# Windowed attention and a SoLU feed-forward layer on one core: the feed-forward layer's middle tensor is transposed by DMA instead of by the tensor engine, its mean moves into the output weights, and the loads of q, k and v go ahead of the weights

## The chip, the cores and the metric

The kernel runs on one core of a Trainium2 chip. That core has five engines with queues of their own, which run in order and wait for each other by semaphores: TensorE (PE; its weight loads are listed apart as PEld), VectorE (DVE), ScalarE (ACT), GpSimd (POOL) and SyncE (SP), which here does nothing but issue DMAs. The metric is the device time of one execution in microseconds (us); lower is better.

## The reference

Attention over 4 batches x 8 heads, 768 positions, head dimension 64, in which a query sees the first 8 keys and the 96 keys up to its own; then a layer over the 3072 tokens, with d_model 512 and d_ff 1024:

```python
h = x @ w_in                               # x: attention output, 3072 x 512
e = np.exp(h - h_max)
sm = e / (np.sum(e, axis=-1, keepdims=True) + 1e-09)
solu = h * sm
mu = np.mean(solu, axis=-1, keepdims=True)
var = np.mean((solu - mu) ** 2, axis=-1, keepdims=True)
ln = (solu - mu) / np.sqrt(var + 1e-06) * g_ln
return (ln @ w_out).astype(np.float32)
```

## The kernel before

Everything is written as one Python program; a scheduler then puts the instructions of each engine into an order and inserts the semaphore waits. Tiles come from pools, and a tile's `bufs` says how many copies of it rotate; an instruction that writes a copy waits until the last reader of its old contents is done. Pools that are closed hand their memory to later pools, with the same kind of wait.

Three stages follow each other.

- **Weights** (lines 104 to 118). SP loads `w_in32` and `w_out32` (2 MB each, fp32) and the 1024 gains `g32`; DVE casts `w_in` to f16 and multiplies `w_out` by the gains in eight pieces (line 115). Both fp32 tiles are in the pool `wtmp`, which is closed before the attention's pools open.
- **Attention** (lines 122 to 298). Eight groups of four heads. Per group SP loads q, k and v (12 DMAs of 192 KB), ACT casts q and k (147, 149), PE transposes them into `pqQ` and `pqK` (157, 159), DVE copies these out (164, 165). `psg` (196, 201) are the scores against the global keys of four heads, `eg` their exponentials. Per head, `psb` (230) are the scores of the local band, `eb` their exponentials (ACT 238) times a mask (DVE 249), `psav` (263) the product with v, `rl` and `onrm` (279, 285) the division by the sum, `pxt` (291) a transpose, and `xT` (295) the copy into the transposed f16 input of the next stage. `psb` and `psg` share one PSUM buffer; `psav` and `pxt` share three.
- **Feed-forward** (lines 300 to 386). 24 tiles of 128 tokens. Per tile: `ph` = x @ w_in (8 matmuls, 313), `e` = exp (ACT 322) with its row sum `s0`, `solu` = e * (1024 / s0) * ph (DVE 328), its square sum (DVE 336), the subtraction of the mean (`smc`, DVE 342), eight PE transposes into `lT` (348), a copy out of PSUM (`lTs`, ACT 352), `po` = the product with the weights (8 matmuls, 355), and a copy of `po` into `ouall` (ACT 359). The normalisation is the same for a whole row, so it is put off: after the last tile the 24 columns of variances go through one square root and one reciprocal (361 to 378), and only then are the 24 tiles scaled (DVE 382) and stored by SP (386).

## Time before, and its profile

| | |
|---|---|
| runs | 334.45, 337.81 and 337.94 us, median 337.81 us |
| span of the profiled execution | 335.8 us |
| PE busy | 247.5 us, 74% of the span |
| DVE busy | 191.3 us, 57% |
| ACT busy | 144.8 us, 43% |
| POOL busy | 28.9 us, 9% |
| DMA | 29.65 MB, 88 GB/s over the span |

The span is the time from the first to the last instruction of one profiled execution; the timed median is 2.0 us longer than it. The stages are found in the trace by their first instructions: the first load of q at 18.94 us, the first `ph` matmul at 197.07 us, the first output store at 312.6 us.

### The profile page before, as it was taken

To read this page: it belongs to the slowest core of one execution; us is meant where nothing else is said; L and a number is where in the kernel's file an instruction comes from. 1 tells how busy PE (TensorE), PEld (TensorE's weight loads), DVE (VectorE), ACT (ScalarE), POOL (GpSimd) and SP (SyncE) were. 2 spreads that over 40 slices of the span, in tenths; PEclk is the share of its full clock that TensorE was granted. 3 is DMA by queue.
4 is the path that set the end of the run, shared out by engine and by line. 5 is a ranking of instruction groups with operands and counts; after the bars stand their busy time and mean duration, and the time that the engine had idled before them with its cause. 6 is when DMAs were issued, how large, how long until landed. Compare 5 with 4: busy or idle time off the path is not lost.

```text
span 335.8 us, 4686 instructions
## 1 busy us (share of the span) xinstructions
PE 247.5 (74%) x1760; PEld 140.0 (42%) x1760; DVE 191.3 (57%) x450; ACT 144.8 (43%) x179; POOL 28.9 (9%) x94
## 2 busy tenths in 40 slices
PE   0005797996969789798897887999889898895400
PEld 0002454664646466564664533444444444442100
DVE  1523364572756656364464528685965957865653
ACT  4012652536544363651634304655565656554100
POOL 7002101121101211110100000000000000000000
PEclk9999999999995755555555559999999999997755
DMA  7679966662777665368000000000000000000586
GB/s 273 227 143 217 196 125 126 127 127 47 142 143 141 142 126 107 60 133 164 2 0 0 2 0 0 2 0 2 2 0 2 0 0 2 0 0 1 197 302 250
DMA packets 81349, 29.65 MB, mean 88 GB/s; under 512 B 76720, under 2 KB 76720, under 8 KB 81328
## 3 DMA queue, kind: packets, MB, share of 16 engines
q1 hardware_dynamic: 81328, 29.37, 38.4%
q8 instruction: 13, 0.21, 0.3%
q14 instruction: 8, 0.07, 0.1%
HBM read 23.07 MB, written 6.29 MB: 87 GB/s over the span
## 4 chain that ended last, share of the span: by engine, by line
PE 49%; ACT 18%; DVE 16%; DMA 10%; issue 4%; SPq 2%; DVEq 0%; ACTq 0%
PE psb L230 13%; PE po L355 9%; PE psav L263 8%; ACT eb L238 7%; PE pxt L291 6%; DVE solu L328 6%; DMA out_dram<-osb 4%; DMA g<-in_moe_g_ln_dram 4%; ACT lTs L352 3%; PE pqK L159 3%; PE pqQ L157 3%; PE psg L196 3%; DVE sq L336 3%; ACT e L322 3%; PE ph L313 2%
## 5 line engine op out<-in xcount | busy, mean ns | idle before, releaser
L238 ACT ACTIVATE eb<-psb 128x1536 f16<-128x1536 f32 x32 | 46.4, 1451 | 52.0 <-PE psb L230 51.7
L230 PE MATMUL psb<-qTt,kTt 64*128 64x256 f16 x192 | 45.6, 395 | 18.9 <-ACT eb L238 15.0
L313 PE MATMUL ph<-w_in_sb,xT 128*128 128x512 f16 x192 | 49.9, 394 | 7.2 <-DVE solu L328 6.6
L355 PE MATMUL po<-gw_out_sb,lTs 128*128 128x512 f16 x192 | 48.4, 398 | 5.0 <-ACT lTs L352 3.8
L249 DVE TENSOR_TENSOR eb<-eb,bmask 128x1536 f16<-128x1536 f16 x32 | 30.5, 952 | 19.3 <-ACT eb L238 19.3
L230 PEld LDWEIGHTS <-kTt 64*128 64x128 f16 x192 | 22.0, 125 | 34.8 <-issue 26.5
L157 PE MATMUL pqQ<-ident,qq 128*128 128x128 f16 x96 | 14.9, 309 | 27.1 <-ACT qq L147 27.1
L355 PEld LDWEIGHTS <-lTs 128*128 128x128 f16 x192 | 17.9, 101 | 39.0 <-ACT lTs L352 20.1
L328 DVE SCALAR_TENSOR_TENSOR solu<-e,r,ph 128x1024 f16<-128x1024 f16 x24 | 30.7, 1280 | 2.7 <-DVE r L325 0.3
L322 ACT ACTIVATE e<-ph 128x1024 f16<-128x1024 f32 x24 | 24.6, 1027 | 15.7 <-PE ph L313 15.6
L359 ACT CAST ouall<-po 128x512 f16<-128x512 f32 x24 | 14.1, 586 | 36.7 <-PE po L355 36.7
L336 DVE CUSTOM_DVE_ANT_0 sq<-solu 128x1024 f16<-128x1024 f16 x24 | 29.2, 1216 | 0.0
L291 PE MATMUL pxt<-ident,onrm 128*64 128x128 f16 x192 | 26.1, 305 | 2.2 <-DVE onrm L285 2.1
L313 PEld LDWEIGHTS <-xT 128*128 128x128 f16 x192 | 18.4, 101 | 22.1 <-issue 5.5
L352 ACT COPY lTs<-lT 128x1024 f16<-128x1024 f16 x24 | 24.3, 1011 | 7.2 <-PE lT L348 7.2
L279 DVE RECIPROCAL rl<-psav 128x6 f32<-128x6 f32 x32 | 6.3, 196 | 33.5 <-PE psav L263 33.3
L263 PE MATMUL psav<-vo,eb 128*128 128x65 f16 x352 | 25.1, 243 | 0.0
L295 DVE COPY xT<-pxt 64x768 f16<-64x768 f16 x32 | 17.6, 549 | 12.7 <-PE pxt L291 12.6
L291 PEld LDWEIGHTS <-onrm 128*64 128x64 f16 x192 | 18.7, 159 | 14.2 <-DVE onrm L285 9.3
L263 PEld LDWEIGHTS <-eb 128*128 128x128 f16 x352 | 20.9, 130 | 7.8 <-issue 4.4
L147 ACT CAST qq<-qq 128x768 f16<-128x768 f32 x16 | 13.2, 824 | 22.7 <-DMA qq<-in_q_dram 22.7
L157 PEld LDWEIGHTS <-qq 128*128 128x128 f16 x96 | 9.4, 137 | 32.4 <-ACT qq L147 29.9
(63 smaller groups left out, 253.5 us busy)
## 6 DMA issues: line engine op xcount, KB each, us to landing
qq<-in_q_dram SPq DMA_DIRECT2D x32, 192.0 KB, 3.9
kk<-in_k_dram SPq DMA_DIRECT2D x32, 192.0 KB, 4.2
v<-in_v_dram SPq DMA_DIRECT2D x32, 192.0 KB, 3.8
out_dram<-osb SPq DMA_DIRECT2D x24, 256.0 KB, 2.0
w_in<-in_moe_w_in_dram SPq DMA_DIRECT2D x1, 2048.0 KB, 7.9
w_out<-in_moe_w_out_dram SPq DMA_DIRECT2D x1, 2048.0 KB, 13.9
g<-in_moe_g_ln_dram SPq DMA_DIRECT2D x1, 4.0 KB, 13.7
```

The source lines that it names most:

```text
L157: nc.tensor.transpose(out=pqQ[:, a, :], in_=qq16[:, a, :], identity=ident)
L230: nc.tensor.matmul(out=psb[:, cj, :], lhsT=kT[:, ts(cj, P)], rhs=qTp[:, ds(P * cj, NQB)], start=st, stop=not st,)
L238: nc.scalar.activation(out=eb.rearrange("p a f -> p (a f)"), in_=psb.rearrange("p a f -> p (a f)"), func=AF.Exp, scale=inv_sqrt_d,)
L249: nc.vector.tensor_tensor(out=eb.rearrange("p a f -> p (a f)"), in0=eb.rearrange("p a f -> p (a f)"), in1=bm_ap, op=ALU.mult,)
L263: nc.tensor.matmul(out=psav[:, rb, :], lhsT=lhs, rhs=rhs_ap, start=st, stop=last, tile_position=tp,)
L291: nc.tensor.transpose(out=pxt[0:D, rb, :], in_=onrm[:, rb, :], identity=ident,)
L313: nc.tensor.matmul(out=ph[:, ds(fh * 512, 512)], lhsT=xT[:, j, ts(tb, P)], rhs=w_in_sb[:, j, ds(fh * 512, 512)], start=(j == 0), stop=(j = ...
L322: nc.scalar.activation(out=e, in_=ph, func=AF.Exp, accum_out=s0)
L328: nc.vector.scalar_tensor_tensor(out=solu, in0=e, scalar=r, in1=ph, op0=ALU.mult, op1=ALU.mult, accum_out=s1,)
L336: nc.vector.tensor_tensor_reduce(out=sq, in0=solu, in1=solu, scale=1.0, scalar=0.0, op0=ALU.mult, op1=ALU.add, accum_out=s2all[:, tb : tb ...
L352: nc.scalar.copy(out=lTs, in_=lT)
L355: nc.tensor.matmul(out=po, lhsT=lTs[:, u, :], rhs=gw_out_sb[:, u, :], start=(u == 0), stop=(u == NFC - 1),)
```

## The change

- The loads of the first group's q, k and v come first on SP; the weights are loaded behind them, by a function that is called after that group's loads and transposes have been written down. `w_in` is now loaded by POOL's DMA queue, which casts to f16 on the way, so DVE's cast goes. `wtmp` is open beside the attention's pools.
- The mean is taken out of the weights instead of out of each token. After the gains are multiplied in (in fp32, in place), eight fp32 matmuls of `w_out32` with a matrix of 1/1024 (`meanw`) give every column's mean `pm`, and one DVE instruction over 128 x 4096 subtracts it and writes `gw_out_sb`. Each column of the weights then sums to zero over d_ff, so that a constant taken from a row of `solu` drops out of the product, and `smc` is not computed.
- Per tile, `u` = e * ph without the division; its square sum is taken by ACT (`sq`, line 353). `u` is transposed by one DMA issued by SP (`uT`, line 356): no transposes on PE, no copy `lTs` on ACT. The division by `s0` goes into the scale of the row.
- The tiles are taken in blocks of six (`GT`). After the sixth, four small DVE instructions and one POOL power (-0.5) give the six columns of scales `rs`. The second half of a tile (`ffn_out`: `po`, then ACT's scaled copy `osb`, then a store issued by ACT's DMA queue) runs six tiles behind the first.
- `ph` has three buffers instead of two, `uT` nine, `u`, `e`, `sq` and `osb` three each.

The diff, cut to its core (the removed lines stand in the functions above):

```diff
+    def load_weights():
+        w_out32 = wtmp.tile([P, NFC, D_MODEL], FP32, name="w_out32")
+        nc.sync.dma_start(out=w_out32, in_=moe_w_out.rearrange("(j p) c -> p j c", p=P))
+        g8 = wtmp.tile([NFC, P], FP32, name="g8")
+        nc.sync.dma_start(out=g8, in_=moe_g_ln.rearrange("(j p) -> j p", p=P))
+        nc.gpsimd.dma_start(out=w_in_sb, in_=moe_w_in.rearrange("(j p) f -> p j f", p=P))
...
+        nc.tensor.transpose(out=pg, in_=g8, identity=id8)
+        g32 = wtmp.tile([P, NFC], FP32, name="g32")
+        nc.vector.tensor_copy(g32, pg)
         for j in range(NFC):
             nc.vector.tensor_scalar_mul(
-                out=gw_out_sb[:, j, :], in0=w_out32[:, j, :],
+                out=w_out32[:, j, :], in0=w_out32[:, j, :],
                 scalar1=g32[:, j : j + 1],
             )
+        pm = apsum.tile([P, D_MODEL], FP32, name="pm", space=bass.MemoryType.PSUM,
+                        tag="out", bufs=3)
+        for j in range(NFC):
+            nc.tensor.matmul(out=pm, lhsT=meanw, rhs=w_out32[:, j, :],
+                             start=(j == 0), stop=(j == NFC - 1))
...
+        nc.vector.tensor_tensor(out=gw_out_sb, in0=w_out32, in1=pm_b,
+                                op=ALU.subtract)
...
+                if b == 0 and gi == 0:
+                    load_weights()
...
+        def ffn_in(tb, st):
+            i = tb % GT
+            ph = mpsum.tile([P, D_FF], FP32, name="ph", space=bass.MemoryType.PSUM,
+                            bufs=3)
...
+            nc.scalar.activation(out=e, in_=ph, func=AF.Exp,
+                                 accum_out=st[0][:, i : i + 1])
+            u = msb.tile([P, D_FF], FP16, name="u")
             nc.vector.scalar_tensor_tensor(
+                out=u, in0=e, scalar=1.0, in1=ph,
+                op0=ALU.mult, op1=ALU.mult, accum_out=st[1][:, i : i + 1],
             )
             sq = msb.tile([P, D_FF], FP16, name="sq")
+            nc.scalar.activation(out=sq, in_=u, func=AF.Square,
+                                 accum_out=st[2][:, i : i + 1])
+            uT = mut.tile([P, NFC, P], FP16, name="uT")
+            nc.sync.dma_start_transpose(out=uT, in_=u)
...
+            nc.gpsimd.tensor_tensor(out=rs, in0=t3, in1=nhalf, op=ALU.pow)
...
+        def ffn_out(tb):
+            uT = uTs.pop(tb)
+            po = mpsum.tile([P, D_MODEL], FP32, name="po", space=bass.MemoryType.PSUM)
+            for c in range(NFC):
+                nc.tensor.matmul(
+                    out=po, lhsT=uT[:, c, :], rhs=gw_out_sb[:, c, :],
+                    start=(c == 0), stop=(c == NFC - 1),
                 )
             osb = msb.tile([P, D_MODEL], FP32, name="osb")
+            nc.scalar.activation(out=osb, in_=po, func=AF.Copy,
+                                 scale=rss[tb // GT][:, tb % GT : tb % GT + 1])
+            nc.scalar.dma_start(out=out[ts(tb, P), :], in_=osb)
+
+        for n in range(NT + GT):
+            if n < NT:
+                if n % GT == 0:
+                    st = [stat.tile([P, GT], FP32, name=f"s{m}") for m in range(3)]
+                ffn_in(n, st)
+                if n % GT == GT - 1:
+                    rss[n // GT] = norm_scale(st)
+            if n >= GT:
+                ffn_out(n - GT)
```

Where the scheduler puts the moved instructions is not to be read from the diff. In the rows below, the names in brackets are what the instruction waits for: an engine, or one of the DMA lanes (DMAHW0 to 7) that the hardware queues' DMAs take in turn, so that every eighth DMA waits for the one eight before it.

On SP, at the start of the program, before:

```order
L108 DMA w_in_109<-in_moe_w_in_dram 128x4x1024
L111 DMA w_out_112<-in_moe_w_out_dram 128x8x512
L113 DMA g_114<-in_moe_g_ln_dram 128x8x1
L137 DMA qq_142<-in_q_dram 128x6x64 [waits DMAHW1_49,DMAHW2_49,DMAHW0_49,DVE_49]
L141 DMA kk_143<-in_k_dram 128x6x64
L137 DMA qq_142<-in_q_dram 128x6x64
```

and now, from the ninth DMA of that queue (the eight ahead of it are q, k and v, without a wait):

```order
L155 DMA qq_167<-in_q_dram 128x6x64 [waits DMAHW0_49]
L159 DMA kk_168<-in_k_dram 128x6x64 [waits DMAHW1_49]
L197 DMA v_196<-in_v_dram 128x6x64 [waits DMAHW2_49]
L197 DMA v_202<-in_v_dram 128x6x64 [waits DMAHW4_49,DMAHW3_49,Pool_49]
L109 DMA w_out_208<-in_moe_w_out_dram 128x8x512
L111 DMA g_210<-in_moe_g_ln_dram 8x128 [waits DMAHW5_49]
L155 DMA qq_412<-in_q_dram 128x6x64 [waits DMAHW6_49]
```

The first load of q waited for the whole weights stage, DVE's work included; now `w_out` is the thirteenth DMA and the gains the fourteenth.

On DVE, behind the first mask multiplication of head 0, before:

```order
L249 TENSOR_TENSOR eb<-eb,bmask 128x1536 [waits DVE_49,Activation_49]
L279 RECIPROCAL rl<-psav 128x6 [waits PE_49]
L285 TENSOR_TENSOR onrm<-psav,rl 128x384 [waits DVE_49]
L249 TENSOR_TENSOR eb<-eb,bmask 128x1536 [waits Activation_49]
L295 COPY xT<-pxt 64x768 [waits PE_49]
```

and now, in the same place, where the next row after the last is head 0's `rl`:

```order
L270 TENSOR_TENSOR eb<-eb,bmask 128x1536 [waits Activation_49] x2
L121 COPY g_219<-pg 128x8 [waits PE_49]
L123 TENSOR_SCALAR w_out_208<-w_out_208,g_219 128x512 [waits DMAHW4_49,DVE_49]
L123 TENSOR_SCALAR w_out_208<-w_out_208,g_219 128x512 x7
L270 TENSOR_TENSOR eb<-eb,bmask 128x1536 [waits Activation_49]
L205 COPY vg_411<-vo_443 8x65 [waits Pool_49]
L205 COPY vg_411<-vo_449 8x65 [waits Pool_49]
L134 TENSOR_TENSOR gw_out_sb<-w_out_208,pm 128x4096 [waits PE_49]
```

On PE, now, the end of head 2's `psb`, half of head 3's, and then head 0's `psav` (before, head 0's `psav` followed on head 1's `psb`, and no weights stood between):

```order
L251 MATMUL psb<-qTt,kTt 128x256 [waits Pool_49]
L119 MATMUL pg<-id_213,g_210 128x8 [waits DMAHW5_49]
L251 LDWEIGHTS kTt
L251 MATMUL psb<-qTt,kTt 128x256 [waits Activation_49]
L251 LDWEIGHTS kTt
L251 MATMUL psb<-qTt,kTt 128x256
L251 LDWEIGHTS kTt
L251 MATMUL psb<-qTt,kTt 128x256
L130 MATMUL pm<-w_out_208,meanw 128x512 [waits DMAHW4_49,DVE_49]
L130 MATMUL pm<-w_out_208,meanw 128x512 [waits DVE_49] x7
L284 LDWEIGHTS eb
L284 MATMUL psav<-vo_157,eb 128x65
```

The scores of the first four heads have moved ahead of the weights' arithmetic, and the rest of these heads behind it, on PE and on DVE.

On ACT, in the middle of the feed-forward stage, before:

```order
L322 ACTIVATE e,s_2872<-ph 128x1024
L359 CAST ouall<-po 128x512
L352 COPY lTs<-lT 128x1024
L359 CAST ouall<-po 128x512
L352 COPY lTs<-lT 128x1024
```

and now, one tile and the beginning of the next (the numbers of the tiles are n for `e` and `sq`, n - 6 for `osb` and the store):

```order
L345 ACTIVATE e,s_2516<-ph 128x1024 [waits PE_49]
L387 ACTIVATE osb<-po,rs 128x512 [waits DMAHW0_49,PE_49]
L389 DMA out_dram<-osb 128x512 [waits DMAHW6_49,Activation_49]
L353 ACTIVATE sq,s_2518<-u 128x1024 [waits DVE_49]
L345 ACTIVATE e,s_2516<-ph 128x1024 [waits PE_49]
```

ACT's order is now a fixed round of four steps in which `sq` of a tile stands between its `e` and the next tile's. PE alternates 8 `po` and 8 `ph` matmuls from tile 7 on.

## Rows read from the trace of the kernel before

**Rows 1.** The page's first line and its chain that ended last.

```profile
span 335.8 us, 4686 instructions
...
PE 49%; ACT 18%; DVE 16%; DMA 10%; issue 4%; SPq 2%; DVEq 0%; ACTq 0%
```

**Rows 2.** The chain in order of time: start us, us, what.

```profile
1.84 13.71 DMA g<-in_moe_g_ln_dram
15.65 3.27 DVE gw_out_sb L115 x8
...
56.23 1.45 PE psb L230 x6
...
197.07 3.61 PE ph L313 x8
200.83 1.12 ACT e L322 x2
...
208.18 1.73 PE po L355 x8
...
218.34 1.13 ACT e L322 x2
...
231.74 1.13 ACT e L322 x2
...
313.04 2.33 DMA out_dram<-osb
```

**Rows 3.** The timeline, start of attention: start us, us, instruction [idle before].

```profile
19.94 0.55 SPq L137 DMA_DIRECT2D qq<-in_q_dram  x1
...
28.37 0.84 SPq L137 DMA_DIRECT2D qq<-in_q_dram  x1
...
40.06 0.20 DVE L279 RECIPROCAL rl<-psav 128x6 f32<-128x6 f32 x1 [1.69 <-PE psav L263]
```

**Rows 4.** The page's DMA issues: KB each, median us from issue to landing.

```profile
qq<-in_q_dram SPq DMA_DIRECT2D x32, 192.0 KB, 3.9
...
w_in<-in_moe_w_in_dram SPq DMA_DIRECT2D x1, 2048.0 KB, 7.9
w_out<-in_moe_w_out_dram SPq DMA_DIRECT2D x1, 2048.0 KB, 13.9
```

**Rows 5.** Groups of instructions by form: busy us, mean ns of one | idle before.

```profile
L328 DVE SCALAR_TENSOR_TENSOR solu<-e,r,ph 128x1024 f16<-128x1024 f16 x24 | 30.7, 1280 | 2.7 <-DVE r L325 0.3
...
L322 ACT ACTIVATE e<-ph 128x1024 f16<-128x1024 f32 x24 | 24.6, 1027 | 15.7 <-PE ph L313 15.6
...
L285 DVE TENSOR_TENSOR onrm<-psav,rl 128x384 f16<-128x384 f32 x32 | 17.8, 555 | 0.8
...
L359 ACT CAST ouall<-po 128x512 f16<-128x512 f32 x24 | 14.1, 586 | 36.7 <-PE po L355 36.7
...
L322 ACT ACTIVATION_READ_ACCUMULATOR e<-ph 128x1 f32 x24 | 4.8, 200 | 0.0
L184 POOL MEMSET vo<- 128x6 f16 x32 | 3.7, 124 | 60.0 <-PE psav L263 60.0
...
L69 POOL TENSOR_SCALAR_AFFINE_SELECT bmask<-bmask 128x2048 f16<-128x2048 f16 x1 | 1.9, 1947 | 1.6 <-ACT bmask L66 1.6
```

**Rows 6.** The timeline at the second tile of the feed-forward stage.

```profile
203.16 1.02 ACT L322 ACTIVATE e<-ph 128x1024 f16<-128x1024 f32 x1 [1.22 <-PE ph L313]
```

**Rows 7.** The timeline's last arithmetic instruction.

```profile
332.19 0.49 DVE L382 TENSOR_SCALAR osb<-ouall,rstdall 128x512 f32<-128x512 f16 x1 [0.21 <-DMA out_dram<-osb]
```

**Rows 8.** The tile `osb`: what stores it, ns min/median/max of the issue.

```profile
L386 SPq DMA_DIRECT2D out_dram<-osb x24: 332/332/440, 312.6 to 332.7; - x24
```

**Rows 9.** Windows: stretch, length, busy us of PE, PEld, DVE, ACT, POOL; PEclk (1.00 is full); DMA.

```profile
118.00:197.00 79.00, 67.89 (x554) 44.05 (x553) 43.25 (x91) 33.20 (x31) 7.32 (x26) 0.50 0.33 63
197.00:202.00 5.00, 4.93 (x12) 1.79 (x13) 0.04 (x2) 1.11 (x2) 0.00 (x0) 0.50 0.00 0
202.00:302.00 100.00, 91.87 (x533) 42.64 (x531) 73.16 (x182) 57.13 (x89) 0.00 (x0) 1.00 0.00 1
```

More of the change, by code (lines that the diff above doesn't have):

```diff
@@ L298 @@
                     )
[L300 removed]
+    GT = 6
     with tc.tile_pool(name="mpsum", bufs=2, space=bass.MemoryType.PSUM) as mpsum, \
          tc.tile_pool(name="msb", bufs=3) as msb, \
[L303 to L310 removed]
+         tc.tile_pool(name="mut", bufs=GT + 3) as mut, \
+         tc.tile_pool(name="stat", bufs=3) as stat:
+        nhalf = stat.tile([P, GT], FP32, name="nhalf", bufs=1)
+        nc.gpsimd.memset(nhalf, -0.5)
+        uTs, rss = {}, {}
+        st = None
+        def ffn_in(tb, st):
+            i = tb % GT
+            ph = mpsum.tile([P, D_FF], FP32, name="ph", space=bass.MemoryType.PSUM,
+                            bufs=3)
             for j in range(NCC):
@@ L341 @@
-            smc = msb.tile([P, D_FF], FP16, name="smc")
-            nc.vector.tensor_scalar(
-                out=smc, in0=solu, scalar1=muall[:, tb : tb + 1], scalar2=LNSC,
-                op0=ALU.subtract, op1=ALU.mult,
-            )
-            lT = mpsum.tile([P, NFC, P], FP16, name="lT", space=bass.MemoryType.PSUM)
-            for u in range(NFC):
-                nc.tensor.transpose(
-                    out=lT[:, u, :], in_=smc[:, ts(u, P)], identity=ident
-                )
-            lTs = msb.tile([P, NFC, P], FP16, name="lTs")
@@ L352 @@
-            nc.scalar.copy(out=lTs, in_=lT)
-            po = mpsum.tile([P, D_MODEL], FP32, name="po", space=bass.MemoryType.PSUM)
-            for u in range(NFC):
-                nc.tensor.matmul(
-                    out=po, lhsT=lTs[:, u, :], rhs=gw_out_sb[:, u, :],
-                    start=(u == 0), stop=(u == NFC - 1),
-                )
-            nc.scalar.copy(out=ouall[:, tb, :], in_=po)
-        nc.vector.tensor_scalar_mul(out=s2all, in0=s2all, scalar1=1.0 / D_FF)
-        nc.vector.tensor_tensor(out=varall, in0=muall, in1=muall, op=ALU.mult)
```

83 lines of the change are left out of this document (28 added, 55 removed).

## The prediction

> **What bounds the kernel now.** I read the page's chain first, then the chain in order of time, which cuts the span of 335.8 us [rows 1] into four parts, and then asked in each part what ends last.
>
> Up to 18 us it is the weights. The gains, third DMA of SP, land at 15.55 us, DVE's eight scalings of `w_out` take 3.27 us more [rows 2], and only then does SP issue the first load of q; its third load goes out at 19.94 us [rows 3], where the third DMA of the queue went out at 1.84 us [rows 2]. PE does nothing until then. From there to 197.07 us is attention, a chain that alternates between PE, ACT and DVE (PE alone is 49% of the whole chain [rows 1]). From 197.07 us it is the feed-forward stage: `e` of every third tile starts 231.74 - 218.34 = 13.40 us after the last such one [rows 2], 4.47 us a tile, through ACT, DVE, PE and ACT again in turn. PE is busy for 91.9 of 100 us in it [rows 9]. From 313 us on it is the 24 stores, up to 335.8: the last scaling starts at 332.19 us [rows 7], and 3.1 us pass from its end to the span's. So feed-forward and stores together take 335.8 - 197.1 = 138.7 us, and that is where most of the change lies.
>
> **The start: 18 us earlier, most of it given back.** The loads go out 19.94 - 1.84 = 18.1 us earlier. The weights are now inside attention, on its path. I follow them.
>
> `w_out` takes the thirteenth place on SP, which was issued at 28.37 us [rows 3], so now at 10.3 us. Landing: 13.9 us, as it took beside `w_in` before [rows 4], so 24.2 us. It has `w_in` beside it again, from POOL's queue. Bounds: 7.9 us, what `w_in` took [rows 4], if it gets the larger share, so 18.2 us; and 13.9 + 3.9 us, if the loads ahead of it are still under way (a load of q takes 3.9 us [rows 4]), so 28.1 us. PE's `pg` waits for the gains behind it and DVE's copy of `pg` for PE, some 0.9 us, then come the scalings, the first of which lets `pm` start at 25.1 us.
>
> `pm` is eight fp32 matmuls of 512 columns, and the trace has none in fp32. In f16, eight of them take 1.73 us at the full clock and 3.61 us at the half [rows 2, 9]. Low end: nothing but the last one behind the last scaling, 28.6 us. High end: both operands are twice as wide, and if each has to be fed in halves, that makes four products, at half clock 14.4 us, so 39.5 us. I take 7 us, which is two products at the half clock or four at the full one: 32.1 us.
>
> Then the subtraction over 4096 columns with one operand in PSUM: 4 x 1.28 = 5.1 us by `solu` (1024 columns, also one operand in PSUM), or 4096/384 x 0.555 = 5.9 us by `onrm` [rows 5]. I take 5.1 us as the nearer in length. Head 0's `rl`, queued behind it on DVE, runs at 37.2 us, where it ran at 40.06 us [rows 3]: of 18.1 us, 2.9 are left. Bounds 33.7 - (24.2 - 18.2) = 27.7 us and 28.1 + 0.9 + 14.4 + 5.9 = 49.3 us.
>
> But some work has been done meanwhile. Before, 56.23 - 40.06 = 16.2 us passed from this `rl` to the first `psb` of group 1 [rows 2, 3]. Of that, two heads' `psb` (1.45 us each [rows 2]) are now done but for half of one, with their exponentials on ACT; on the other hand group 2's first q and k are now transposed in this stretch and not later. I take 14 us, so group 1's `psb` at 51.2 us, 5.0 earlier than before, plus some 1.6 us for the transposes that group 1 no longer has to do. The other seven groups hold the same instructions as before. The feed-forward stage then starts at 197.07 - 6.6 = **190.5 us**; with the bounds, 16 us earlier to 5 us later than before.
>
> **Feed-forward.** Gone for a tile: eight transposes on PE, `lTs` on ACT, `sq`, `smc` and three small instructions on DVE. Added: `sq` on ACT, a DMA transpose, ACT's issue of the store. What the units then need:
>
> PE: 16 matmuls, 2 x 1.73 = 3.46 us at the full clock [rows 2, 9].
>
> ACT: a round of `e`, `osb`, store, `sq`. `e` takes 1.03 us, and 0.2 us for its sum's read that overlaps by half: `solu`'s chain shows 1.12 us [rows 2, 5]. `u` (1.28 us, 0.09 for its sum, as `solu`) then runs on DVE, and `sq`, which I price as `e` since it has the same length and a sum too, waits for it. So a round is 1.12 + 0.05 + 1.37 + 0.05 + 1.12 = **3.7 us**, as long as `osb` and the store fit into the 1.4 us that ACT waits for `u`: `osb` as `ouall`, 0.59 us [rows 5], and the issue 0.33 us as on SP [rows 8] (or 0.84, as for a load among many [rows 3]), so 0.9 to 1.4 us; they fit. The round is above PE's 3.46, so this exchange between ACT and DVE becomes the bound, at 3.7 us instead of 4.47.
>
> The DMA transpose has no row. A tile of `u` is 256 KB; cut into the 256-byte rows of 128 x 128 blocks it is 1024 pieces. The nearest row is the load of q: 768 pieces of 256 bytes, of which SP issues one every 0.84 us [rows 3] and which lands after 3.9 us [rows 4]. So 1.1 us a tile in a stream, and some 5 us to landing. `uT` is wanted six tiles later, 22 us; `u` has three buffers, so the transpose also has to be done some 10 us after its issue. Both cover it: I cost it at nothing. Low end the same nothing; the high end is a rival below.
>
> The page "DMA: Bandwidth & Descriptors" of the Trainium skill (section "Latency and other measured facts") gives a measured 261 GB/s for a DMA transpose, by which I estimate 1.0 us a tile, and the sum would stay as it is; "Advanced Engine Details and Errata" of the Trainium skill (section "DGE: Hardware vs Software") speaks against the change, since it calls a transpose issued by a hardware queue, as here, the less efficient kind. No run here shows either yet.
>
> The sum from the stage's start: `e` of tile 0 at 3.8 us (200.83), of tile 1 at 6.1 us (203.16 [rows 6]; the matmuls are at the half clock there [rows 9]). Tiles 2 to 6 have no second half: ACT alternates `sq` and `e`, 2.24 us a tile, tile 6 at 17.3 us. The first block's scales come in here (`sq` of tile 5, two small DVE steps, POOL's power, `osb` of tile 0): tile 7 at 21.6 us. Then 16 rounds of 3.65 to 3.7, tile 23 at 80.5 us. Its `u` ends 2.5 us later, `sq` 1.2, two DVE steps 0.5, the power 0.6 (between 0.12 us for POOL's smallest instruction and 1.95 for a large one [rows 5]). Then six tiles are still to be scaled; two have their `po` ready, four follow at PE's 1.8 us, the last `osb` ends 8.2 us later. With the 3.1 us to the end, 80.5 + 4.8 + 8.2 + 3.1 = **96.6 us** against 138.7. Bounds: 94 us (shorter issue, no gap at the blocks) and 106 us (issue 0.84, the power 2 us at each block, `osb` at 0.7).
>
> **The sum.** 190.5 + 96.6 = 287.1 us of span; with the 2.0 us by which the median (337.8) is above the profiled span, **289 us**.
>
> **Rivals.**
>
> A. The forecast: 181 + 94 + 2 = 277 us to 202.5 + 106 + 2 = 310.5 us by the bounds, most likely 281 to 303: chance 0.72.
>
> B. The transposes flow slower than ACT's round. If the crossbar moves pieces smaller than 256 bytes at the load's 0.84 us / 768 = 1.1 ns a piece, pieces of 64 bytes make 4.5 us a tile: 24 x 4.5 + 6 before the first + 9 behind the last = 123 us, total 315 us. Chance 0.11.
>
> C. The same, further: pieces of 32 bytes make 9 us a tile, 24 x 9 + 15 = 231 us, total 424 us, slower than before. It decides from where 24 tiles, 15 us and 190.5 pass 335.8 us: 5.4 us a tile. For it speaks that nothing in the trace shows such a transfer, and that nothing of the store's large packets carries over; against it, that the queue holds one DMA per tile and that the pieces in `u` are contiguous. Chance 0.12.
>
> D. The clock. In attention's second half PE is busy for 67.9 of 79 us and has the half clock; at 202 us, after 4.93 busy us of 5, the clock rises [rows 9]. If it stayed at the half clock, a tile would take PE 2 x 3.61 = 7.2 us, 17 tiles 60 us more: 349 us. Against it: at that clock the feed-forward's PE has no gaps, and the one such stretch in the trace ended in the rise. Chance 0.03. That gaps lower PE's clock and steady work raises it is also what "TensorE: Matmul & The Clock Gate" of the Trainium skill says (section "HAM oscillation — how this bites in real kernels"); the trace agrees in the direction.
>
> E. The earlier loads gain nothing, since `pm` and the subtraction come later still: that is the far end of A's bounds and is counted there.
>
> **How the numbers follow.** The likeliest is A with 289 us. A's far ends and B hold the rest of the upper side: 278 to 320 us holds about 0.97 of A and more than half of B, 0.77 or so, and to reach further up would only buy the thin space before C. A measurement of this kernel tells about 1% from no change. Faster by over 1%, below 334.4 us: A and B, 0.83. Slower: C and D, 0.15. Between: 0.02.
>
> **What would show it.** First load at about 1 us; `w_out` landing near 24 us; a gap on PE between head 3's `psb` and head 0's `psav` in which only `pm` runs; `rl` of head 0 near 37 us; `ph` near 190 us; `e` every 3.7 us, with ACT waiting for DVE's `u` and not for PE or a DMA; DMA transposes landing some 5 us after issue; no stores after the end but the last six tiles'. It would be wrong if `po` waits for `uT` or `u` for a transpose (B, C), if ACT's issue of the stores holds up `sq`, if `pm` takes much more than 7 us, or if the granted clock in the second half is 0.50.

## The result, and the profile after

The changed kernel takes 286.14 us (median of 4 runs, 285.64 to 287.89) against 337.88 us (4 runs, 334.45 to 337.99): a ratio of 0.851 with a 95% interval of 0.845 to 0.857, or 51.7 us less. The forecast was 289 us with a range of 278 to 320. The profiled execution took 286.56 us, its span is 284.9 us. All readings below are from that one, and answer to the span of 335.8 us of before.

The page's first line, the shares of its chain, and three of its DMA issues (KB each, median us to landing; for the transpose, to landing only):

```profile
span 284.9 us, 4203 instructions
...
PE 62%; ACT 15%; issue 9%; DVE 7%; SPq 2%; DMA 2%; POOL 1%; POOLq 0%; ACTq 0%
...
out_dram<-osb ACTq DMA_DIRECT2D x24, 256.0 KB, 2.1
w_out<-in_moe_w_out_dram SPq DMA_DIRECT2D x1, 2048.0 KB, 14.5
...
uT<-u SPq DMA_TRANSPOSE x24, 3.1
```

PE now carries 62% of the chain, where it was 49% [rows 1], and the DMA transposes are in no step of it. The time went in three places. Each is the difference of two starts in the two traces:

| part | before | after | less |
|---|---|---|---|
| span's start to the first `e` (loads, attention) | 200.83 | 194.01 | 6.8 |
| first `e` to the 24th | 301.89 - 200.83 = 101.1 | 266.05 - 194.01 = 72.0 | 29.0 |
| 24th `e` to the span's end | 335.8 - 301.89 = 33.9 | 284.9 - 266.05 = 18.9 | 15.1 |

**The start.** The timeline of after, where [rows 2, 3] stood before (start us, us, engine, instruction, idle before it):

```profile
0.81 0.45 SPq L155 DMA_DIRECT2D qq<-in_q_dram  x1
...
10.15 4.45 SPq L109 DMA_DIRECT2D w_out<-in_moe_w_out_dram  x1
...
26.55 0.80 PE L251 MATMUL psb<-qTt,kTt 64*128 64x256 f16 x3 [1.25 <-ACT eb L259]
...
27.28 8.70 PE L130 MATMUL pm<-w_out,meanw 128*128 128x512 f32 x16
...
36.01 4.42 DVE L134 TENSOR_TENSOR gw_out_sb<-w_out,pm 128x4096 f16<-128x4096 f32 x1 [5.12 <-PE pm L130]
...
40.35 0.19 DVE L300 RECIPROCAL rl<-psav 128x6 f32<-128x6 f32 x1
...
52.64 1.44 PE L251 MATMUL psb<-qTt,kTt 64*128 64x256 f16 x6 [0.25 <-ACT eg L228]
```

The loads start 18 us earlier, but head 0's `rl` runs at 40.35 us, where it ran at 40.06 [rows 3]. The weights stand in between: `w_out` lands at 24.65 us, `pm` cannot start before 27.28, since half of head 3's `psb` is in front of it and waits for ACT; it takes 8.70 us, and DVE's subtraction 4.42 more. So at this point all of the 18 us is gone. Group 1's first `psb`, the last row, stood at 56.23 us [rows 2] and is 3.6 us earlier; by the start of the feed-forward stage 6.8 us are there again.

**The feed-forward stage.** A round is 3.445 us. The window from 220 to 260 us (length, busy us and instructions of PE, PEld, DVE, ACT, POOL, then PE's clock, DMA share, GB/s), and one round of ACT and DVE:

```profile
220.00:260.00 40.00, 40.00 (x187) 18.12 (x185) 14.60 (x30) 31.01 (x57) 2.65 (x2) 1.00 0.63 154
```

```profile
262.60 1.00 ACT L345 ACTIVATE e<-ph 128x1024 f16<-128x1024 f32 x1
...
263.60 0.68 ACT L387 ACTIVATE osb<-po,rs 128x512 f32<-128x512 f32 x1
263.73 1.22 DVE L348 SCALAR_TENSOR_TENSOR u<-e,ph 128x1024 f16<-128x1024 f16 x1 [2.21 <-ACT e L345]
264.30 0.34 ACTq L389 DMA_DIRECT2D out_dram<-osb  x1
...
264.99 1.06 ACT L353 ACTIVATE sq<-u 128x1024 f16<-128x1024 f16 x1 [0.72 <-DVE u L348]
...
266.05 1.00 ACT L345 ACTIVATE e<-ph 128x1024 f16<-128x1024 f32 x1
```

Two things have the same length. PE has no gap in 40 us, and its 16 matmuls of a tile take 2 x 1.73 = 3.46 us. ACT, in the order in which its instructions stand, starts `e`, then waits until DVE's `u` is there, then does `sq`: 1.13 to `u`'s start, 1.26 to `sq`, 1.06 to the next `e`, 3.45 us. In this trace the chain that ended last runs over PE's matmuls without a break from 190.26 to 226.94 us, and from the second block's scales on over ACT and DVE: at a block's border ACT waits for the power on POOL before `osb`, and there the round is 4.1 us.

```profile
228.77 0.69 ACT L387 ACTIVATE osb<-po,rs 128x512 f32<-128x512 f32 x1 [0.84 <-POOL rs L375]
```

The two are so nearly equal that the trace alone does not say which of them sets the round.

**The tail**, in the timeline:

```profile
270.15 1.32 POOL L375 TENSOR_TENSOR rs<-t,nhalf 128x6 f32<-128x6 f32 x1 [20.09 <-DVE t L373]
271.51 1.26 ACT L387 ACTIVATE osb<-po,rs 128x512 f32<-128x512 f32 x2 [1.92 <-POOL rs L375]
...
272.25 8.75 PE L382 MATMUL po<-gw_out_sb,uT 128*128 128x512 f16 x32 [2.59 <-ACT osb L387]
```

The last block's scales come at 271.5 us. Until then both buffers of `po` are full and PE waits 2.59 us; four tiles are still to be multiplied, and they take 8.75 us, 2.2 us a tile in place of 1.73. The granted clock is 0.50 from 272.8 to 276.2 us, behind PE's wait, and 1.00 after that; over the window from 260 us on it is 0.89.

### The profile page after: what moved, and what is told of

The parts are those of the page before. It is cut to its first block, busy times and chain, and to the rows that moved or that the text cites. A ratio compares the mean times of both kernels' runs of the same rounds, so it can differ in the third digit from the quotient of the medians.

```text
span 284.9 us, 4203 instructions
## 1 busy us (share of the span) xinstructions
PE 241.1 (85%) x1585; PEld 135.5 (48%) x1585; DVE 135.8 (48%) x291; ACT 146.7 (52%) x201; POOL 34.3 (12%) x100
## 3 DMA queue, kind: packets, MB, share of 16 engines
q1 hardware_dynamic: 101664, 27.28, 49.2%
## 4 chain that ended last, share of the span: by engine, by line
PE 62%; ACT 15%; issue 9%; DVE 7%; SPq 2%; DMA 2%; POOL 1%; POOLq 0%; ACTq 0%
PE psb L251 15%; PE psav L284 10%; PE ph L337 9%; PE pxt L312 8%; PE po L382 7%; ACT eb L259 7%; ACT e L345 4%; PE pqQ L175 3%; PE pm L130 3%; PE pqK L177 3%; PE psg L217 3%; ACT eg L228 2%; DMA qq<-in_q_dram 2%; DVE gw_out_sb L134 2%; DVE u L348 1%
## 5 line engine op out<-in xcount | busy, mean ns | idle before, releaser
L251 PE MATMUL psb<-qTt,kTt 64*128 64x256 f16 x192 | 47.3, 407 | 15.5 <-ACT eb L259 12.7
L348 DVE SCALAR_TENSOR_TENSOR u<-e,ph 128x1024 f16<-128x1024 f16 x24 | 29.3, 1222 | 45.0 <-ACT e L345 45.0
L382 PE MATMUL po<-gw_out_sb,uT 128*128 128x512 f16 x192 | 46.4, 390 | 3.7 <-ACT osb L387 3.7
L337 PE MATMUL ph<-w_in_sb,xT 128*128 128x512 f16 x192 | 46.4, 392 | 0.6 <-DVE xT L316 0.6
L382 PEld LDWEIGHTS <-uT 128*128 128x128 f16 x192 | 19.2, 100 | 28.0 <-issue 6.6
L353 ACT ACTIVATE sq<-u 128x1024 f16<-128x1024 f16 x24 | 25.4, 1058 | 10.7 <-DVE u L348 9.9
L312 PEld LDWEIGHTS <-onrm 128*64 128x64 f16 x192 | 19.4, 164 | 18.0 <-DVE onrm L306 12.1
L316 DVE COPY xT<-pxt 64x768 f16<-64x768 f16 x32 | 17.6, 549 | 17.4 <-PE pxt L312 17.2
L228 ACT ACTIVATE eg<-psg,gbias 128x768 f16<-128x768 f32 x8 | 7.2, 900 | 35.2 <-PE psg L222 35.2
L284 PEld LDWEIGHTS <-eb 128*128 128x128 f16 x352 | 20.6, 129 | 8.5 <-issue 4.8
L387 ACT ACTIVATE osb<-po,rs 128x512 f32<-128x512 f32 x24 | 16.2, 680 | 10.4 <-PE po L382 6.2
L203 POOL CAST vo<-v 128x384 f16<-128x384 f32 x32 | 17.3, 547 | 14.8 <-DMA v<-in_v_dram 14.7
L306 DVE TENSOR_TENSOR onrm<-psav,rl 128x384 f16<-128x384 f32 x32 | 17.8, 555 | 0.7
```

Source lines behind the costliest of these rows:

```text
L251: nc.tensor.matmul(out=psb[:, cj, :], lhsT=kT[:, ts(cj, P)], rhs=qTp[:, ds(P * cj, NQB)], start=st, stop=not st,)
L284: nc.tensor.matmul(out=psav[:, rb, :], lhsT=lhs, rhs=rhs_ap, start=st, stop=last, tile_position=tp,)
L306: nc.vector.tensor_tensor(out=onrm, in0=psav[:, :, 0:D], in1=rl_b, op=ALU.mult)
L312: nc.tensor.transpose(out=pxt[0:D, rb, :], in_=onrm[:, rb, :], identity=ident,)
L337: nc.tensor.matmul(out=ph[:, ds(fh * 512, 512)], lhsT=xT[:, j, ts(tb, P)], rhs=w_in_sb[:, j, ds(fh * 512, 512)], start=(j == 0), stop=(j = ...
L348: nc.vector.scalar_tensor_tensor(out=u, in0=e, scalar=1.0, in1=ph, op0=ALU.mult, op1=ALU.mult, accum_out=st[1][:, i : i + 1],)
```

## The experiments

Twelve kernels were run. All are edits of the changed kernel; e11 is e3b with one edit more, and e12 and e13 join edits of the others. The theory: (a) the round fell because PE lost its transposes and `po`, six tiles behind, waits for nothing; (b) the tail fell because the stores no longer stand in a row behind the last tile; (c) of the 18 us at the start most was lost to the fold of the mean. The rivals were that (b) brought nearly all, that the lag or the fold was worth nothing, or that ACT set the round.

| kernel | median us (range) | ratio to before, 95% interval |
|---|---|---|
| changed kernel | 286.14 (285.64 to 287.89) | 0.851 (0.845 to 0.857) |
| e1_pe_transpose | 295.36 (294.62 to 295.73) | 0.886 (0.880 to 0.893) |
| e2_no_fold | 281.68 (278.32 to 284.51) | 0.840 (0.828 to 0.853) |
| e3_stores_last | 285.63 (284.18 to 286.51) | 0.857 (0.850 to 0.864) |
| e4_weights_later | 285.30 (283.47 to 286.07) | 0.856 (0.849 to 0.863) |
| e3b_scale_at_end | 298.62 (297.81 to 299.60) | 0.891 (0.887 to 0.895) |
| e10_order_ahead | 279.84 (276.84 to 282.46) | 0.832 (0.825 to 0.839) |
| e5_sq_dve | 286.50 (284.76 to 287.20) | 0.854 (0.849 to 0.859) |
| e6_half_po | 271.33 (269.01 to 272.95) | 0.811 (0.805 to 0.817) |
| e7_gt3 | 282.16 (280.61 to 284.25) | 0.833 (0.827 to 0.838) |
| e11_lag_one | 309.63 (308.00 to 311.33) | 0.914 (0.908 to 0.919) |
| e12_no_fold_ahead_gt3 | 282.32 (280.80 to 283.28) | 0.832 (0.827 to 0.837) |
| e13_ahead_gt3 | 276.34 (275.96 to 277.00) | 0.815 (0.812 to 0.819) |

The kernel before scatters by 1 to 3% within a group of runs beside them (330.6 to 340.4 us over the three groups, with medians of 334.6, 335.1 and 338.6 us), the changed kernels by 0.4 to 2.2%, e2 the most; so differences among these are taken from their medians and from the traces, and one of 2 or 3 us between medians of different groups shows little by itself.

**e1: the transposes back on PE.**

```diff
+            lT = mpsum.tile([P, NFC, P], FP16, name="lT", space=bass.MemoryType.PSUM)
+            for c in range(NFC):
+                nc.tensor.transpose(out=lT[:, c, :], in_=u[:, ts(c, P)], identity=ident)
             uT = mut.tile([P, NFC, P], FP16, name="uT")
-            nc.sync.dma_start_transpose(out=uT, in_=u)
+            nc.vector.tensor_copy(out=uT, in_=lT)
```
(`ph` has two buffers instead of three, to make room in PSUM.)

> The changed kernel with the middle layer transposed on TensorE again (eight transposes of a tile into one PSUM tile, copied to SBUF by VectorE) in place of the DMA transpose; everything else, the folded mean and the store of each tile at once among it, stays. Theory: the feed-forward stage is set by TensorE at 3.455 us a tile (ph 1.73 + po 1.73), tied with the chain of e and u on ScalarE and VectorE at 3.445; eight transposes more, by the old kernel some 0.6 us a tile, come on top, so the round is 4.0 to 4.2 us and 24 tiles give 13 to 18 us: about 301 us (297 to 306). Rival, that the gain of the stage comes from the stores and the statistics and the transposes were covered all along: no more than 2 us, about 287.

It took 295.4 us, 9.2 more, just under the expected range. The window from 220 to 260 us, and three rows of one round:

```profile
220.00:260.00 40.00, 40.00 (x244) 19.50 (x242) 20.82 (x39) 29.48 (x53) 2.65 (x2) 1.00 0.18 68
```

```profile
228.20 1.02 ACT L345 ACTIVATE e<-ph 128x1024 f16<-128x1024 f32 x1
...
230.63 0.62 PE L357 MATMUL lT<-ident,u 128*128 128x128 f16 x8
...
232.16 1.02 ACT L345 ACTIVATE e<-ph 128x1024 f16<-128x1024 f32 x1
```

PE again has no gap, and the round is 3.96 us: 0.51 longer for eight transposes that take 0.62 us with the overlap at both ends. So the transposes were not covered, and the DMA transpose gives back what they cost PE. It is less than the 13 to 18 us expected: from first to last `e` 10.7 us were added, but the tail is 1.2 us shorter and the stage starts 1.1 us earlier. Of the 10.7, 4.2 fall on the first six steps from `e` to `e` (16.3 us for 12.1), where the third `ph` buffer is missing too; the two are not told apart there.

**e2: no fold.** `pm` and the subtraction go; DVE takes each tile's mean off `u` instead:

```diff
...
+            nc.vector.tensor_scalar(
+                out=uc, in0=u, scalar1=mu, scalar2=None, op0=ALU.subtract)
-            nc.sync.dma_start_transpose(out=uT, in_=u)
+            nc.sync.dma_start_transpose(out=uT, in_=uc)
```

> The changed kernel without the fold of the mean into the output weights: no fp32 matmuls pm and no subtraction at the start; VectorE takes each tile's mean and subtracts it before the DMA transpose. Theory: of the 18 us by which the loads come earlier, the fold's 8.7 us of fp32 matmuls and 4.4 us of subtraction give most back, since they stand ahead of heads 0 to 3's second half; without them the stage starts 8 to 12 us earlier, and the extra VectorE work (two passes of 128x1024 in f16, under 2 us a tile) stays below the round of 3.45: about 276 us (273 to 280). Rival, that the start is held by something else (the order of heads 0 to 3, the softmax's exponentials): within 3 us of the changed kernel, 283 to 289; second rival, that the mean's passes lengthen the round on VectorE: 290 or more with a round above 3.6 us.

281.7 us, between the theory's range and the first rival's; the round stayed at 3.445. The stage began 4.9 us earlier, not 8 to 12. Where the rest went is seen in the first `rl` of the first four head groups, of the changed kernel and of e2:

```profile
40.35 0.19 DVE L300 RECIPROCAL rl<-psav 128x6 f32<-128x6 f32 x1
...
58.25 0.20 DVE L300 RECIPROCAL rl<-psav 128x6 f32<-128x6 f32 x1 [1.69 <-PE psav L284]
...
77.03 0.20 DVE L300 RECIPROCAL rl<-psav 128x6 f32<-128x6 f32 x1 [0.64 <-PE psav L284]
...
95.36 0.20 DVE L300 RECIPROCAL rl<-psav 128x6 f32<-128x6 f32 x1 [0.80 <-PE psav L284]
```

```profile
29.22 0.19 DVE L289 RECIPROCAL rl<-psav 128x6 f32<-128x6 f32 x1
...
50.54 0.20 DVE L289 RECIPROCAL rl<-psav 128x6 f32<-128x6 f32 x1 [1.69 <-PE psav L273]
...
71.82 0.20 DVE L289 RECIPROCAL rl<-psav 128x6 f32<-128x6 f32 x1 [2.12 <-PE psav L273]
...
91.37 0.20 DVE L289 RECIPROCAL rl<-psav 128x6 f32<-128x6 f32 x1 [2.12 <-PE psav L273]
```

At the first `rl` e2 leads by 11.1 us, which is the price of the fold there; then by 7.7, 5.2 and 4.0, and by 2.7 at the fifth to the seventh group. It comes back to 4.9 only in the eighth: there PE's clock is 1.00 from 155.0 to 158.3 us in e2 and 0.50 in the changed kernel. Whether the edit or only this execution made it rise is not shown. Against the kernel before, e2's lead is 10.8 us at the first `rl` and between 9.6 and 11.7 at the seven others, so its groups take as long as before. It is the changed kernel's groups that are shorter, 17.9, 18.8 and 18.3 us against 21.3, 21.3 and 19.6. While PE waited for the weights and did `pm`, ACT and the loads got ahead, and PE then found its work ready, as far as the waits tell: in the changed kernel it waits for ACT's `eb` ahead of `psb` for 0.4 us between 58 and 95 us (the first row), and for 3.8 us between 114 and 155 (the second); e2 waits for 3.5 us between 51 and 91 (waits: us, times, longest).

```profile
PE psb L251 <- ACT eb L259: 0.4, 1, 0.4
...
PE psb L251 <- ACT eb L259: 3.8, 4, 1.5
```

```profile
PE psb L240 <- ACT eb L248: 3.5, 3, 1.5
```

**e4: the weights in the middle.** `load_weights` is called at `b == 2` in place of `b == 0`.

> The changed kernel with the loading, scaling and folding of the weights moved behind head group 2's start, in the middle of attention; the fold is kept. Theory: the 8.7 us of pm and the 4.4 us of subtraction leave the start, but TensorE has them at the half clock in attention (about 13.7 us); attention is held by the exponentials on ScalarE with TensorE partly idle there, so some of it is hidden: 276 to 286 us, 281 taken. Rival, that attention has TensorE as its bound: all 13.7 us come back and the time is 286 to 292 us.

285.3 us, within the changed kernel's scatter, and inside the theory's range only at its end. Its `rl` at the groups around the fold:

```profile
86.25 0.20 DVE L300 RECIPROCAL rl<-psav 128x6 f32<-128x6 f32 x1 [2.12 <-PE psav L284]
...
123.34 0.19 DVE L300 RECIPROCAL rl<-psav 128x6 f32<-128x6 f32 x1
...
141.24 0.20 DVE L300 RECIPROCAL rl<-psav 128x6 f32<-128x6 f32 x1 [1.69 <-PE psav L284]
...
160.03 0.20 DVE L300 RECIPROCAL rl<-psav 128x6 f32<-128x6 f32 x1 [0.64 <-PE psav L284]
...
176.11 0.20 DVE L300 RECIPROCAL rl<-psav 128x6 f32<-128x6 f32 x1 [0.93 <-PE psav L284]
```

The same pattern a second time, elsewhere. Up to 86 us e4 leads the kernel before by 15.3 to 17.7 us: nearly the whole of the earlier loads is kept as long as no weights are in the way. The group with the fold takes 37.1 us in place of 20.6, and the three after it 17.9, 18.8 and 16.1; the lead over before goes from 15.3 to -2.2 and back to 7.9 us. So it is the weights' scaling and fold, wherever they stand, that take the shift away, and the groups behind them return some of it.

**e3: the stores last.** `osb` is held and the 24 stores are written behind the loop.

> The changed kernel with every output tile held in SBUF and all 24 stores issued after the last tile. Theory: a store that follows its tile is free, and 24 stores in a row at the end cost what the kernel before showed from its last scaling to its end, 15 to 20 us less the 2 to 3 of the one store that ends the changed kernel: about 300 us (296 to 306). Rival, that the 16 DMA engines take the stores side by side, so only the issue counts (24 x 0.34 us on one queue): about 293 us or less.

285.6 us, and it says nothing on the theory: the scheduler put each store behind its `osb` again (at 220.16, 221.25 and 224.69 us, between ACT's steps of the running stage). It is a repeat of the changed kernel. The order of the source did not bind the scheduler here; a dependence of the data does. Hence the next one.

**e3b: scaling at the end, forced by the data.**

```diff
...
-            nc.scalar.activation(out=osb, in_=po, func=AF.Copy,
-                                 scale=rss[tb // GT][:, tb % GT : tb % GT + 1])
-            nc.scalar.dma_start(out=out[ts(tb, P), :], in_=osb)
+            raw = hold.tile([P, D_MODEL], FP32, name=f"raw{tb}")
+            nc.scalar.copy(out=raw, in_=po)
...
+        rs = norm_scale(st)
+        for tb in range(NT):
+            osb = msb.tile([P, D_MODEL], FP32, name="osb")
+            nc.vector.tensor_scalar_mul(out=osb, in0=raws[tb],
+                                        scalar1=rs[:, tb : tb + 1])
+            nc.sync.dma_start(out=out[ts(tb, P), :], in_=osb)
```

> e3_stores_last had its stores put back behind their tiles by the scheduler, so it tested nothing; here the data force them to the end. The unscaled output tiles are held in SBUF in f32, the row statistics are worked out once over all 24 tiles after the last one (as in the old kernel), and then VectorE scales and SyncE stores 24 tiles in a row. Theory: the old kernel took 22.8 us from its first scaling (313.04) to its end (335.8), against 3.9 us from the changed kernel's last scaling to its end, so about 19 us come back, less what ScalarE saves: about 304 us (299 to 309). Rival, that the old end was slow only because its VectorE scalings were and the stores run side by side: 292 us or less.

298.6 us, 12.5 more, just under the expected range. Its end in the timeline:

```profile
268.53 4.20 POOL L376 TENSOR_TENSOR rs<-t,nhalf 128x24 f32<-128x24 f32 x1 [108.60 <-DVE t L374]
272.77 1.28 DVE L399 TENSOR_SCALAR osb<-raw,rs 128x512 f32<-128x512 f32 x3 [4.32 <-POOL rs L376]
273.28 21.23 SPq L401 DMA_DIRECT2D out_dram<-osb  x24
...
293.67 0.49 DVE L399 TENSOR_SCALAR osb<-raw,rs 128x512 f32<-128x512 f32 x1 [0.22 <-DMA out_dram<-osb]
```

From the first scaling to the span's end (297.3) it is 24.5 us. In the kernel before it was 23.9: its first scaling runs at 311.95 us, and the 313.04 of the expectation is the first store on the chain [rows 2].

```profile
311.95 1.28 DVE L382 TENSOR_SCALAR osb<-ouall,rstdall 128x512 f32<-128x512 f16 x3
```

In both, DVE waits for stores to free its three buffers. So the row of stores costs what was thought, and (b) holds. But 12.5 and not 19 us come on top, because without the scales no `po` waits: the first scaling is there at 272.8 us, when the changed kernel still has four tiles to multiply.

**e11: `po` one tile behind.** e3b with `ffn_out(n - 1)` in place of `ffn_out(n - GT)`.

> e3b_scale_at_end with po written one tile behind ph in place of six; nothing else differs, since there no po waits for scales. Theory: the six tiles of lag are what keeps TensorE from waiting for a tile's own e, u and DMA transpose (2.3 us, then 1.3 of issue and 3.1 to landing, 6.7 us in all, against 1.7 us for one ph); with one tile of lag the scheduler can put at most the third ph buffer in between, so a round grows from 3.45 to 4 to 5 us: 310 us or more (308 to 330), where e3b took 298.6. Rival, that the lag is worth nothing and the gain of the round comes from the transposes alone: 297 to 301.

309.6 us, 11.0 more than e3b. From first to last `e` it takes 82.8 us, e3b 71.4. The waits of PE and of its weight loads from 215 to 265 us (us, times, longest):

```profile
PE po L383 <- DMA uT<-u: 1.6, 6, 0.4
```

```profile
PEld L383 <- DMA uT<-u: 7.4, 11, 0.9
```

e3b has no wait of either kind there. The transpose lands 3.1 us after its issue here, 3.0 in e3b. So it is free only because several tiles lie between `u` and `po` (six here; e7 below tries three); the change's order of the work is about as much of the gain as the transposes that left PE. Neither e1 nor e11, with 82.8 us each from first to last `e`, comes back to the 101.1 of the kernel before; what the work that left DVE and ACT (`smc`, `lTs`, the small steps) gave was not run by itself.

**e5 and e6: ACT or PE?** e5 gives `sq` back to DVE; e6 lets `po` take four of eight matmuls (half of the sum over the middle layer is left out of its output).

```diff
-            for c in range(NFC):
+            for c in range(NFC // 2):
...
```

> The changed kernel with the square sums taken on VectorE again, as in the old kernel; ScalarE then has 1.06 us a tile less in the feed-forward stage. Theory: TensorE (3.455 us a tile) sets that round by itself, so only the first seven tiles, where ScalarE alternates e and sq at 2.04 us a tile, can gain: 283 to 287 us. Rival, that the chain over ScalarE and VectorE (3.445) is what holds TensorE: round down to some 2.6 us and 268 us or less.

> The changed kernel with four of the eight po matmuls of each tile left out (half of the sum over the middle layer is missing from the output), so TensorE has 2.6 us a tile in place of 3.455. Theory: ScalarE's and VectorE's round of 3.445 is tied with TensorE's and holds alone as well: the stage stays within 2 us, and only the six po at the end shorten, by 6 x 0.9 us: 279 to 284 us. Rival, that TensorE alone set the round: down to what the e and sq need on ScalarE, 2.0 to 2.7 us a tile plus the stores, 268 us or less.

e5 took 286.5 us with a round of 3.45 in its steady part: relief for ACT alone buys nothing. PE has no gap there from 220 to 260 us, and now `e` does wait for PE, 31.7 us in all, where it was 9.5 in the changed kernel:

```profile
L345 ACT ACTIVATE e<-ph 128x1024 f16<-128x1024 f32 x24 | 24.6, 1024 | 32.3 <-PE ph L337 31.7
```

e6 took 271.3 us, at 2.8 us a tile: under the theory's 279 to 284 and over the rival's 268. The theory fell, but the trace shows that more than PE's work changed:

```profile
228.22 1.01 ACT L345 ACTIVATE e<-ph 128x1024 f16<-128x1024 f32 x1
...
229.78 1.03 ACT L345 ACTIVATE e<-ph 128x1024 f16<-128x1024 f32 x1
...
230.78 1.07 ACT L353 ACTIVATE sq<-u 128x1024 f16<-128x1024 f16 x1
...
232.20 1.06 ACT L353 ACTIVATE sq<-u 128x1024 f16<-128x1024 f16 x1 [0.26 <-DVE u L348]
...
233.82 1.01 ACT L345 ACTIVATE e<-ph 128x1024 f16<-128x1024 f32 x1
```

With a shorter PE the scheduler ordered ACT anew: two `e`, then two `sq`, so that DVE's `u` runs beside the second `e`, and two tiles take 5.6 us, with ACT busy for 37.7 of the 40 us from 210 to 250. ACT's chain is 3.45 us only in the order that the changed kernel has; in another order it needs 2.8. The bound that no order removes is therefore PE's 3.46, by e5, e6 and e1 together; e6 alone does not show what the old order of ACT would have done with less on PE.

**e7: blocks of three.** `GT = 3` in place of 6.

> The changed kernel with blocks of three tiles for the statistics in place of six, so that po runs three tiles behind ph. Theory: the tail of the changed kernel (18.85 us from the last e to the end) holds a wait of TensorE for the last block's scales: with two po buffers it stands still 2.59 us before 272.25, and six tiles are left to scale when the scales come at 271.5; with three tiles left the tail loses 3 to 5 us, and four more of POOL's powers (1.32 us) run beside other work: about 282 us (280 to 284). Rival, that three tiles of lag no longer hide the DMA transpose (1.3 us of issue, 3.1 to 5.6 to landing, behind 2.3 of e and u) or that the block borders hold up ScalarE: 287 us or more.

282.2 us, 4.0 less, as expected; but the trace gives the edit a smaller part. The power takes 0.85 us on three columns instead of 1.32 on six, fewer tiles are left behind it, and from the 24th `e` to the end it is 278.9 - 267.37 = 11.5 us in place of 18.9. Of these 7.3 us, first to last `e` takes back 4.9 (76.9 us for 72.0), since `ph` runs only three tiles ahead and there are twice as many block borders. So stage and tail are 2.4 us shorter. The other 3.6 us of this execution lie ahead of the stage, which starts at 190.43 us (first `e`), where the order of PE is unchanged: PE's clock was 1.00 there from 50 to 56 us and 0.84 from 105 to 110, where the changed kernel's trace shows 0.50. Three tiles of lag still hide the transpose but for 3.0 us of waiting weight loads.

**e10, e12, e13: the order in attention.** From e2 came the idea that the order of PE's instructions makes the groups between 40 and 95 us short. e10 writes the next group's loads, casts and transposes ahead of the present group's heads, and its global block ahead of the last head:

```diff
...
+            for op, i in [('p', 0), ('h', 0), ('p', 1), ('h', 1), ('h', 2), ('g', 0), ('h', 3)]:
+                if op == "h":
+                    head(state, eg, i)
+                elif nxt and op == "p":
+                    prep(nxt, i)
+                elif nxt:
+                    eg2 = glob(nxt)
...
```

> The changed kernel with the same work, written in another order: each head group's loads, casts and transposes ahead of the heads of the group before, and its global block (psg, eg) ahead of the last head of the group before. The fold stays at the start. Reason: the lead of e2_no_fold over the changed kernel shrank from 11.1 us at the first rl to 2.7 at the fifth group, because the changed kernel's groups between 40 and 114 us took 18.3 to 18.8 us and those of e2_no_fold 19.6 to 21.3; on TensorE the two have the same instructions in another order (two scores in a row, psb twice, in the slow groups). Theory: the order is the cause, and with the interleaved order in all groups the last four, now 20.9 to 21.3, take 18.5, so about 10 us less: 276 us (272 to 281). Rival, that the period is set by the work or by the loads: 284 to 288.

279.8 us, 6.3 less, and the stage starts 5.8 us earlier; but the reason given is not borne out. From `rl` to `rl`, its groups in the middle take 18.4, 20.1, 19.9, 20.1 and 19.9 us, no 18.5. Short are the first such step (16.2 us), for which the preparation had been done while the weights were under way, and the last (15.7), in which no next group is to be prepared. In the last one the clock rises too, behind a stretch in which PE has no gap (windows as above):

```profile
155.00:160.00 5.00, 5.00 (x45) 3.34 (x44) 3.26 (x8) 2.17 (x2) 0.00 (x0) 0.51 0.01 3
160.00:165.00 5.00, 3.33 (x46) 2.20 (x44) 3.26 (x9) 2.35 (x2) 0.00 (x0) 1.00 0.00 0
```

`psb` takes 303 ns each from 159 to 168 us, 409 in the middle of attention. The changed kernel's trace has 0.50 throughout this part. So the order is worth something, by work done ahead and by a denser PE, but it does not make the middle groups shorter.

> The three edits together that each looked worth something: no fold of the mean (e2: 4.6 us less than the changed kernel), the next group's preparation written ahead (e10: 6.3 us less), blocks of three tiles (e7, hoped for 4 us). Theory, if they add up: 286.1 - 4.6 - 6.3 - 4 = 271 us. Rival: e10's gain came from a backlog that the fold had made and is not there without it, then about 278 us.

> e10_order_ahead with blocks of three tiles, the fold kept. Theory: e10's 279.8 less the 3 to 5 us of e7: 276 us (274 to 278). Rival: the blocks of three cost at their borders what they gain at the end: 279 to 281.

e13 is at 276.3 us, 3.5 less than e10, as expected, and the fastest of all, 9.8 us below the changed kernel. Its stage starts 2.4 us earlier than e10's, with the clock at 1.00 from 120 to 125 and from 158 to 163 us, and stage and tail together are 88.4 us (e10 89.1), so not much of it is the blocks of three: up to the stage the two have the same matmuls in the same order, by the tiles' names. e12, without the fold, does not add up: 282.3 us, as much as e7 alone. Its first `rl` is at 28.60 us, its second only at 52.28, and its first `e` at 192.13, 6.3 us behind e13's (185.80), 3.9 behind e10's and 3.0 behind e2's (189.15). So without the fold the new order gains nothing, it even loses. That fits the mechanism of e12's rival, by which the order's gain rests on the backlog that the fold makes, but not its 278 us; the mechanism is argued and not shown. Why attention, with loads and preparation in hand, falls back to 20 us a group was not settled; PE is busy for 69.2 of 80 us from 60 to 140 us in e12, and waits there for `eb` on ACT (5.8 us), then for DVE's `eb` and `onrm` (2.2 and 1.8).

## Why the prediction was right

**The start, right in the sum, by two errors that cancel.** The prediction had the stage's start at 190.5 us; it was 190.26. `w_out`'s issue (10.3, measured 10.15) and landing (24.2, measured 24.65) held, and the subtraction was 4.42 us for 5.1. The term that was too small is `pm`: "7 us, which is two products at the half clock or four at the full one" was 8.70, four products with their first part at the half clock (the durations are in the last section), and it started at 27.28 and not 25.1, as half of head 3's `psb` stood ahead of it and waited for ACT. So "of 18.1 us, 2.9 are left" was wrong; nothing was left. The other error is in what comes back behind it. The stretch to group 1's first `psb` was priced at 14 us and took 12.3 (52.64 - 40.35), group 1 was to save 1.6 us and saved 2.7 (18.8 us from `rl` to `rl` for 21.5), and the other six, which were to keep their length, saved 0.5 together: 7.1 us from the first `rl` to the stage, where 3.7 were forecast. e2 and e4 show both halves. That the sum fits to 0.2 us is luck, and not only for this: eight executions with the same matmuls in the same order up to the stage start it up to 3.7 us apart (last section).

**The round, nearly right in size, the bound half right.** The 3.7 us for ACT's exchange with DVE were 3.445: the overlap between the steps is larger than priced, `osb` (0.68 us) and the store (0.34) fitted, as was said. "This exchange between ACT and DVE becomes the bound" is half right: the chain does run over it from 226.94 us on, but at 3.445 us it is level with PE's 3.46 and not above it, and PE is the bound that e5 leaves and e1 raises.

**The transpose, right.** The prediction said "I cost it at nothing", with 1.1 us a tile in a stream and 5 to landing; it is 1.27 us on the queue (median) and 3.1 to landing (5.6 at most). Rivals B and C are out: no piece of the chain is a transpose. The Trainium skill ("DMA: Bandwidth & Descriptors", section "Latency and other measured facts") gave 261 GB/s, measured with a middle dimension that is not contiguous, an estimate of 1.0 us a tile. No run here sends the transposes back to back, so the rate itself is not shown; one tile in 2.04 us, as in the run-up, held up no `u`. The Trainium skill's page "Advanced Engine Details and Errata" (section "DGE: Hardware vs Software") calls the transposes of hardware queues the less efficient kind; no run here compares the two kinds.

**The run-up and the tail.** `e` of tile 6 came 15.8 us after the stage's start (17.3 predicted), of tile 7 20.6 (21.6), of tile 23 75.8 (80.5). The tail from there was 18.9 us and not 4.8 + 8.2 + 3.1 = 16.1: the power was 1.32 us for 0.6, and the four last `po` 2.2 us for 1.8, at the lower clock that followed PE's wait. Sum: 94.6 us for 96.6: the run-up and the rounds came out 4.7 us shorter and the tail 2.7 longer, which again partly cancel.

**The clock.** Rival D did not come: the granted clock is 0.50 from 190 to 194 us, and 1.00 between 220 and 260.

## What to carry to other kernels

An operation moved to a transfer engine is free only as far as its result is wanted late: here six tiles of lag in place of one were worth 11 us, about as much as the transposes that left TensorE (9.2). Arithmetic that is moved out of the loop onto the weights still has to be placed: it cost 11 us where it stood, and more than half of that came back behind it, most likely since the other engines worked ahead meanwhile; read the lead at several places behind the edit, not at one. And a statement's place in the source need not hold where a scheduler works: it moved the work in e4 and e10 and nothing in e3. To test an order, make the data force it.
